# Batch 0's rotary rotations without their addition: TensorE sums both terms while it transposes, in a new order of the work

## The chip, the cores and the metric

The kernel runs on one core of a Trainium2 chip. The metric is the device time of one execution in microseconds (us). The core has five engines with queues of their own: TensorE (PE in the profile; its weight loads are shown apart, as PEld), VectorE (DVE), ScalarE (ACT), GpSimd (POOL) and SyncE (SP), which here only issues transfers. The profile gives start and duration of every instruction, and what ended each wait.

## The reference

Attention with rotary positions for 4 batches of 8 heads (576 positions, head size 64), and then an MLP with a squared ReLU:

```python
def rotate(x):
    x1, x2 = (x[..., :half], x[..., half:])
    return np.concatenate([x1 * cos - x2 * sin, x1 * sin + x2 * cos], axis=-1)
q_rot, k_rot = (rotate(q), rotate(k))
scores = scale * np.matmul(q_rot, k_rot.transpose(0, 1, 3, 2))
attn = np.exp(scores - np.max(scores, axis=-1, keepdims=True))
attn = attn / (np.sum(attn, axis=-1, keepdims=True) + 1e-09)
x = np.matmul(attn, v)           # then (B, S, H*D)
h = x @ w_in
r = np.maximum(h, 0.0)
out = (s * (r * r) + b) @ w_out
```

All inputs and the output are float32. The weights (512 x 2048 and 2048 x 512) come as 8-byte words, of which the kernel makes float32.

## The kernel before

Two heads of a batch make a pair: 16 pairs, numbers 0 to 3 for batch 0. A pair's q, k and v are loaded (`load_x`, L529) and q and k rotated. Then come, for each tile of query rows, the scores (TensorE), their maximum (VectorE), the exponential with its sum (ScalarE), a division, a transpose of the probabilities and the product with v. The MLP takes units of 256 rows as soon as their attention is there. The pairs of batches 1 to 3 are split into two float16 halves and transposed by DMA; their scores and the MLP of their rows are sums of float16 products.

Batch 0 (`FQ = (0, 1, 2, 3)`) goes another way, since the kernel starts with it: everything stays float32, and TensorE does its transposes. For a pair pr and nm = "k" or "q":

- `rotate` (L581 to L592) has three steps, each an instruction on the whole 128 x 576 tile: z = x * sin with the halves swapped (L588), x = x * cos in place (L590), x = x + z (L592). Which engine does it, VectorE or GpSimd, is in a table; for the eight rotations of batch 0 it is VectorE.
- `qk_T` (L762 to L770) transposes the 128 x 576 tile into a PSUM tile `s`: four 128 x 128 transposes (L766) and, for the last 64 columns, two 64 x 64 products with the unit matrix (L769).
- `qk_ev` copies the PSUM tile to `qkT` in SBUF on ScalarE or VectorE.
- `s_pair` (L653) makes the scores of two tiles, `s_max` (L678) their negative maxima, `s_exp` the exponentials `p`. `p_diag` and `p_T` (L794, L796) transpose and divide the probabilities, by a float32 product with a diagonal matrix.

The weights are made in the same stretch: a load (L440), one or two conversions on ScalarE, GpSimd or VectorE, a join on VectorE (L409, wio<-x), a gram of its columns on TensorE (L493) and its maximum (L496).

`plan()` (L154 on) makes a list of all pieces of work with their dependencies. It sets no order: three strings do. `ORDER` names the pieces in the order in which they are written into the program, two characters each; `PICKS` says which engine does a piece that several could do; `SLOTS` which buffer each tile takes. Every engine works through its own instructions in that order, so a piece that waits holds up what stands behind it on its engine. The buffers that matter here are two PSUM tiles for scores and transposes, and two SBUF tiles for z:

```python
BUFS = {"s": 2, "bank": 2, "po": 1, "nat": 1, "ot": 1, "xc": 4, "xt": 1, "hr": 3, "k": 2, "q": 2, "v": 4, "z": 2, "p": 4, "pab": 6, "pt": 2, "x": 4,
```

Of the kernel before, what the change touches and what calls it, by code (L numbers as in the profile page):

```python
# [7 lines left out]
F32 = mybir.dt.float32  # L8
# [20 lines left out]
B, H, S, D, DM, DFF, P = 4, 8, 576, 64, 512, 2048, 128  # L29
# [9 lines left out]
    "AAC8C9A9AMDYDZAXAyDADBDDDCA_DEDGA-DFANBADIDKAODcA4DHAPBBDJDdAiI9DLDfDMAYDeAZI-A0AaAzDgAnI_A1JFJADiARA5DOA6DhJGDmA7AkDkJB"  # L39
    "DRAcJCAjDSDjA8DlDnJDAlDTBpC-AoDPDWApBCDQASAqDUJHATDvBODXDoJIDwAbDaDVArAmAUJEJOAsAtAdDxACJJDyAVABAeAQJKJRBrBqAfJSJPAgBkJL"  # L40
    "D1BsJQAhBPBIDzDNJTBQC_DpD2D0DbBRD3JUDqBDJVEGJYDrAvAuJWDsAWADDtD4AwJdBeBmBlAEAFJXDuBnBtD5AxECJeBoBTJZBKJgBJD6JfAGBuAHBEBL"
    "A2JhBSBFAIKMBZJiA3JaEFJjBGJkEfEJJMKND_BgKPBfKOJlAJJnBhKQAKBUBVBvD7JsEAKRJmBaKSBWJNJoKWETJvBbCFEgJtJwJbKTBcJuBXJxJ7JpB0Jy"
    "BwKXEDJzEUJcJ0J2BYBxJ8EhKDJ9BdByBiKEBMBHCGCVCHKUKbJ-J1J_CIKAKFD8J3BNCbKGBjKeEIEVD9KcJqJ4B1KfALJ5KYKdEBJrKBK5B2KVKgJ6B3CX"
    "BzKhEQaaCWKiEHK6KHCKaZCYCcacD-CdB_K7abCeKlERCQB4KqadB5KjaeKZKrafKmakKsCLKkKtEKLfKIKaKnCAK8CMalLgKuFVCNELanKvCBEMC2ENKwb0"
    "LhEOamK9EPCCK-KxEEavB6aoLFapESCSKyEWKoCRLSEYayKJK0LGKpaqCTaxLHK1KCCOagC4EXC3CxawK_LTC5ahB8EZCgB7CJLCLULiCPEkLVB9LZEiKKLI"
    "LWLDaiKLKzLJLab1ajazb2b3K2LXLEarLjb4EqLKLra0Eab5a1Erb6asLkLLLsEjatLPL4CmLtElb7K3LMEtMFK4LbLNChCibGLQLAL5MGbJCzEmCjLBMHbI"
# [103 lines left out]
def plan():  # L150
# [32 lines left out]
    def prep(pr):  # L183
# [161 lines left out]
def tile_rope_attention__then__relu2_mlp(  # L345
# [755 lines left out]
```

## Time and profile before

| | |
|---|---|
| median of 3 runs | 589.58 us (588.7 to 591.73) |
| profiled execution, own time | 591.62 us |
| its span, first to last instruction | 589.8 us |
| TensorE busy | 570.6 us (97%), 4621 records |
| VectorE busy | 464.0 us (79%) |
| ScalarE busy | 417.1 us (71%) |
| GpSimd busy | 117.7 us (20%) |

A row of a timeline reads: start, busy time, engine, line, operation, out<-in by the program's names, shape, count of records [idle time of the engine before it, and what ended it]. Rows that follow each other on one line are merged. Matmuls are pipelined, so the busy time of a row reaches beyond the start of the next; the pace of a row is the distance to the next start. "L766 ... x4" is four records: a float32 product is shown as two. A wait is put down to the one that ended it last.

### The profile page before, as it was taken

What the parts mean: (1) busy time and instruction counts of PE and PEld (TensorE: products, weight loads), DVE (VectorE), ACT (ScalarE), POOL (GpSimd) and SP (SyncE); (2) the same over time, 40 slices, a digit from 0 to 9 for tenths busy, and PEclk for the clock granted to TensorE, in tenths of its full rate; (3) what the DMA queues carried; (4) which work ended last, traced back from release to release, by engine and by line L of the source; (5) the groups of instructions that cost most, each with busy time, mean ns of one, the idle gap of its engine ahead of it and who ended that gap; (6) DMA issues with size and microseconds to landing.
All of it is one profiled execution on the core that took longest, in us unless ns stands there. A gap on an engine that the chain in (4) does not pass through costs nothing.

```text
span 589.8 us, 12277 instructions
## 1 busy us (share of the span) xinstructions
PE 570.6 (97%) x4621; PEld 389.3 (66%) x4621; DVE 464.0 (79%) x975; ACT 417.1 (71%) x869; POOL 117.7 (20%) x123
## 2 busy tenths in 40 slices
PE   3799999999999999999999999999999999999997
PEld 2567867666676567666765675667656766666774
DVE  5999999999999999999999999997777464313121
ACT  4789999898999878977878786766456554443422
POOL 0146332224123541211251101201110000010000
PEclk9999999999999999999999999999999999999999
DMA  8999999987776698998647756676440334220100
GB/s 300 345 299 297 243 256 214 191 184 151 155 203 156 122 180 169 222 193 185 168 105 167 186 147 148 151 169 143 101 102 21 82 93 84 57 61 1 37 1 36
DMA packets 210011, 90.32 MB, mean 153 GB/s; under 512 B 192288, under 2 KB 196768, under 8 KB 209952
## 3 DMA queue, kind: packets, MB, share of 16 engines
q1 hardware_dynamic: 209952, 89.54, 63.5%
q8 instruction: 36, 0.59, 0.5%
q14 instruction: 23, 0.19, 0.1%
HBM read 31.97 MB, written 4.72 MB: 62 GB/s over the span
## 4 chain that ended last, share of the span: by engine, by line
PE 91%; DVE 3%; DMA 2%; ACT 2%; issue 1%; SPq 0%; DVEq 0%
PE px L889 29%; PE po L972 27%; PE px L759 9%; PE s L671 8%; PE px L922 4%; PE po L943 4%; PE s L653 3%; PE s L972 2%; DMA st_k<-in_k_dram 2%; PE po L794 1%; PE s L672 1%; PE px L493 1%; PE px L813 1%; DMA pt<-pab 1%; PE s L660 1%
## 5 line engine op out<-in xcount | busy, mean ns | idle before, releaser
L889 PE MATMUL px<-xa,wio 128*128 128x256 f16 x1536 | 179.7, 273 | 0.0
L972 PE MATMUL po<-wio,g 128*128 128x512 f16 x720 | 171.4, 379 | 0.8 <-ACT o L412 0.8
L889 PEld LDWEIGHTS <-wio 128*128 128x128 f16 x1536 | 147.7, 98 | 28.6 <-issue 2.0
L412 ACT ACTIVATE p<-s,nm 128x576 f32<-128x576 f32 x144 | 105.4, 733 | 36.0 <-DVE s L680 23.1
L972 PEld LDWEIGHTS <-g 128*128 128x128 f16 x816 | 75.8, 98 | 74.0 <-issue 3.4
L409 DVE SCALAR_TENSOR_TENSOR pab<-p,sum,pab 128x576 f16<-128x576 f32 x136 | 114.0, 849 | 7.6 <-ACT pab L412 3.7
L680 DVE TENSOR_SCALAR_CACHE_REDUCE s<-s,sc 128x576 f32<-128x576 f32 x108 | 87.9, 818 | 16.8 <-PE s L672 15.7
L406 POOL TENSOR_SCALAR pab<-p,sum 128x576 f16<-128x576 f32 x54 | 48.1, 894 | 240.5 <-DVE sum L708 189.7
L412 ACT ACTIVATE hr<-px,xc 128x512 f32<-128x512 f32 x64 | 43.7, 682 | 52.4 <-PE px L889 52.3
L913 DVE SCALAR_TENSOR_TENSOR g<-hr,xc,g 128x512 f16<-128x512 f32 x64 | 48.4, 761 | 18.8 <-ACT g L412 18.1
L412 ACT ACTIVATE pab<-p,sum 128x576 f16<-128x576 f32 x64 | 48.7, 767 | 11.0 <-DVE sum L708 10.4
L404 DVE TENSOR_SCALAR g<-hr,xc 128x512 f16<-128x512 f32 x24 | 11.9, 497 | 47.9 <-ACT hr L412 32.6
L759 PE MATMUL px<-pt,v 128*64 128x320 f16 (+2 forms) x640 | 48.9, 281 | 0.3 <-DMA pt<-pab 0.2
L412 ACT ACTIVATE hr<-hr 128x512 f32<-128x512 f32 x68 | 42.7, 628 | 1.5
L671 PE MATMUL s<-qkT 128*128 128x512 f16 (+1 forms) x120 | 41.4, 383 | 0.1
L671 PE MATMUL s<-kS,qkT 128*128 128x512 f16 (+1 forms) x120 | 41.3, 380 | 0.0
L412 ACT ACTIVATE g<-hr,xc 128x512 f16<-128x512 f32 x40 | 28.7, 717 | 16.9 <-PE po L972 10.9
L759 PEld LDWEIGHTS <-v 128*64 128x64 f16 x640 | 32.1, 110 | 11.1 <-issue 7.4
L671 PEld LDWEIGHTS <-qkT 128*128 128x128 f16 (+1 forms) x240 | 22.5, 100 | 22.8 <-issue 3.7
L922 PE MATMUL px<-x,wio 128*128 128x128 f32 x256 | 31.4, 278 | 0.0
L922 PEld LDWEIGHTS px<-x,wio 128*128 128x128 f32 x256 | 29.8, 192 | 2.2 <-issue 1.2
L412 ACT ACTIVATION_READ_ACCUMULATOR p<-s,nm 128x1 f32 x144 | 28.2, 196 | 0.0
(154 smaller groups left out, 796.3 us busy)
## 6 DMA issues: line engine op xcount, KB each, us to landing
x<-in_moe_w_in_dram SPq DMA_DIRECT2D x16, 512.0 KB, 5.1
x<-in_moe_w_out_dram SPq DMA_DIRECT2D x16, 512.0 KB, 5.0
st_v<-in_v_dram SPq DMA_DIRECT2D x16, 320.0 KB, 4.1
st_k<-in_k_dram SPq DMA_DIRECT2D x16, 288.0 KB, 3.8
st_q<-in_q_dram SPq DMA_DIRECT2D x16, 288.0 KB, 4.1
out_dram<-o SPq DMA_DIRECT2D x7, 512.0 KB, 4.2
kS<-qkT SPq DMA_DIRECT2D x24, 144.0 KB, 2.5
pt<-pab SPq DMA_TRANSPOSE x152, 2.9
```

Of the source, the lines that this page charges most:

```text
L406: eng.tensor_scalar(out=out, in0=in0, scalar1=s1, scalar2=s2, op0=op0, op1=op1)
L409: nc.vector.scalar_tensor_tensor(out=out, in0=in0, scalar=scalar, in1=in1, op0=op0, op1=op1)
L412: nc.scalar.activation(out=out, in_=in_, func=func, **kw)
L653: nc.tensor.matmul(ps[h][:, to], d["qF"][hh, t * P:(t + 1) * P], d["kF"][hh, keys], start=True, stop=True)
L671: nc.tensor.matmul(ps[rows, MAIN:2 * MAIN], lhs, kk[:, h:8:2], start=(n == 0), stop=(n == 1))
L680: nc.vector.tensor_scalar(out=T["s"], in0=T["s"], scalar1=st[pr]["es"], scalar2=None, op0=ALU.mult, op1=ALU.min, accum_out=T["nm"])
L759: nc.tensor.matmul(o[64 * h:64 * h + 64, c], v_rows(pr, h, k, z), p_rows(pr, 2 * (i // 4) + h)[:, k, c], start=((z, k) == todo[0]), stop=( ...
L889: nc.tensor.matmul(ph, w16[0][:, f, wz, cc], X["xa"][:, xz, c], start=(c == 0 and n == 0), stop=(c == NC - 1 and n == 2))
L913: nc.vector.scalar_tensor_tensor(out=g[:, 1], in0=r, scalar=xs[u]["c"][:, 2:3], in1=g[:, 0], op0=ALU.add, op1=ALU.subtract)
L922: nc.tensor.matmul(ph, wi[:, f + 1, c * P:(c + 1) * P], xs[0]["x"][:, c, j * P:(j + 1) * P], start=(c == 0), stop=(c == NC - 1))
L943: nc.tensor.matmul(X["po"][:, j * DM:(j + 1) * DM], gs["h", j, f - f % 4][:, f % 4 * P:(f % 4 + 1) * P], wo[:, f + 1], start=(n == 1), sto ...
L972: nc.tensor.matmul(po, g[:, gz, jj], w16[1][:, f, wz, to], start=(n == 1 and i == 0), stop=(n == NF and i == 2))
```

## The change

In `plan()` the rotations of batch 0 have two steps in place of three: z and x * cos are made, and x = x + z is not. z is kept as an operand of `qk_T`, which reads both tiles, so the slot of z is held until TensorE has read it. `qk_T` multiplies each block of both by the unit matrix and sums the two in PSUM: eight 128 x 128 products and four 64 x 64 ones, where four transposes and two products stood. The lines behind it move down by three (L766 becomes L768, L769 becomes L772, L794 becomes L797). The rotations of the other batches keep three steps. `ORDER`, `PICKS` and `SLOTS` are new from end to end; a line of each is shown.

```diff
 ORDER = (
-    "AAC8C9A9AMDYDZAXAyDADBDDDCA_DEDGA-DFANBADIDKAODcA4DHAPBBDJDdAiI9DLDfDMAYDeAZI-A0AaAzDgAnI_A1JFJADiARA5DOA6DhJGDmA7AkDkJB"
...
+    "AAC8C9A9AMDUDVAXAyABACADDBDCDEDDA_A-BADGAOANA4DFAPDYBBDaDHDJAQAiDZI1AZDIAYDWI2AzAaI3I9ARA0DcDbI4I-A1I_A6ADI5AnAEAFA5DeI6"
...
 PICKS = (
-    "SSSSSSGSSSGGGVGGVGGVSGVGSSSSSGSSVVSSVVSSVVSSVVSSGSGSVGGSGVVGGSVVGSSGVSSSVGGSSGVSGSVVGGSVVSGSVVGSSVGSVSVVSGSVVSGSSGSSSSSG"
...
+    "GSGGSGGGVVGGVGGGVGGSSGGVSSGSSSSSVVSSVVSSVVVSVVSSGSGGVGGSSVGGSSVVGSGVSSSVGSSSVVGGGVVGGSVVSGGVVSGGVGGSGVGSSGVGGGSSSSSSSVG"
...
 SLOTS = (
-    "000111230101000001010102003011110011011011222130001310002013113020010103100110000101010011223012310100010101110112001121"
...
+    "000111230101000010110100020131011010011102301122030010200113101010323001011200003001010110210302310001100001102011030132"
...
         for nm in "kq":
-            add((DVE, POOL), "rotate", pr, nm, steps=3, r=[("tab",)], w=[(nm, pr), ("z", pr, nm)])
+            add((DVE, POOL), "rotate", pr, nm, steps=2 if F else 3, r=[("tab",)], w=[(nm, pr), ("z", pr, nm)])
         if F:
             for nm in "kq":
-                add(PE, "qk_T", pr, nm, r=[(nm, pr), ("tab",)], w=[("s", ("T", pr, nm))])
+                add(PE, "qk_T", pr, nm, r=[(nm, pr), ("z", pr, nm), ("tab",)], w=[("s", ("T", pr, nm))])
...
-        z = new(rp, "z", [P, 9, 2, 32], F32)
+        z = st[pr]["z", nm] = new(rp, "z", [P, 9, 2, 32], F32)
...
         x, o = d[nm], new(ps_s, "s", [P, 1024], F32)
+        terms = x, d["z", nm].rearrange("p t h e -> p t (h e)")
         for t in range(4):
-            nc.tensor.transpose(o[:, t * P:(t + 1) * P], x[:, 2 * t:2 * t + 2].rearrange("p h d -> p (h d)"), ident)
-        for h in range(2):
-            hh = slice(64 * h, 64 * h + 64)
-            nc.tensor.matmul(o[hh, 512:576], x[hh, 8], ident[hh, hh], start=True, stop=True)
+            for n, y in enumerate(terms):
+                nc.tensor.matmul(o[:, t * P:(t + 1) * P], y[:, 2 * t:2 * t + 2].rearrange("p h d -> p (h d)"), ident, start=not n, stop=bool(n))
+        for n, y in enumerate(terms):
+            for h in range(2):
+                hh = slice(64 * h, 64 * h + 64)
+                nc.tensor.matmul(o[hh, 512:576], y[hh, 8], ident[hh, hh], start=not n, stop=bool(n))
         d["T", nm] = o
```

The new order shows at two places. The first is VectorE's start, from its first rotation on (st_k_109 and st_q_111 are pair 0's k and q, st_k_117 and st_q_119 pair 1's, x the weight blocks, nm the maxima of the first two score tiles). Before:

```order
L588 TENSOR_TENSOR z0_125<-st_k0_109,tab_91 128x9x2x32
L590 TENSOR_TENSOR st_k0_109<-st_k0_109,tab_91 128x576
L588 TENSOR_TENSOR z1_128<-st_q0_111,tab_91 128x9x2x32
L592 TENSOR_TENSOR st_k0_109<-st_k0_109,z0_125 128x576
L590 TENSOR_TENSOR st_q0_111<-st_q0_111,tab_91 128x576
L592 TENSOR_TENSOR st_q0_111<-st_q0_111,z1_128 128x576
L409 SCALAR_TENSOR_TENSOR wio_93<-x0_113,wio_93 128x512
L588 TENSOR_TENSOR z0_154<-st_k1_117,tab_91 128x9x2x32
L409 SCALAR_TENSOR_TENSOR wio_93<-x1_115,wio_93 128x512
L590 TENSOR_TENSOR st_k1_117<-st_k1_117,tab_91 128x576
L588 TENSOR_TENSOR z1_178<-st_q1_119,tab_91 128x9x2x32
L592 TENSOR_TENSOR st_k1_117<-st_k1_117,z0_154 128x576
```

With the change:

```order
L588 TENSOR_TENSOR z0_127<-st_k0_109,tab_91 128x9x2x32
L590 TENSOR_TENSOR st_k0_109<-st_k0_109,tab_91 128x576
L588 TENSOR_TENSOR z1_130<-st_q0_111,tab_91 128x9x2x32
L590 TENSOR_TENSOR st_q0_111<-st_q0_111,tab_91 128x576
L404 TENSOR_SCALAR wio_93<-x0_113 128x512
L409 SCALAR_TENSOR_TENSOR wio_93<-x0_113,wio_93 128x512
L409 SCALAR_TENSOR_TENSOR wio_93<-x1_115,wio_93 128x512
L588 TENSOR_TENSOR z0_169<-st_k1_117,tab_91 128x9x2x32
L588 TENSOR_TENSOR z1_176<-st_q1_119,tab_91 128x9x2x32
L590 TENSOR_TENSOR st_k1_117<-st_k1_117,tab_91 128x576
L678 TENSOR_REDUCE nm0_201<-s0_189 128x1
L409 SCALAR_TENSOR_TENSOR wio_93<-x2_121,wio_93 128x512
```

The additions L592 are gone, two weight blocks are joined ahead of pair 1's rotations, a conversion (L404) has come to VectorE, and pair 1's two z stand next to each other. z0_169 takes the slot of z0_127, z1_176 that of z1_130, and both of those are now read by TensorE.

The second place is TensorE's start. Before:

```order
L766 MATMUL s_133<-ident,st_k_109 128x128 x4
L769 MATMUL s_133<-ident,st_k_109 64x64 x2
L766 MATMUL s_144<-ident,st_q_111 128x128 x4
L769 MATMUL s_144<-ident,st_q_111 64x64 x2
L493 LDWEIGHTS wio
```

With the change, the first call alone:

```order
L768 MATMUL s_132<-ident,st_k_109 128x128
L768 MATMUL s_132<-ident,z_127 128x128
L768 MATMUL s_132<-ident,st_k_109 128x128
L768 MATMUL s_132<-ident,z_127 128x128
L768 MATMUL s_132<-ident,st_k_109 128x128
L768 MATMUL s_132<-ident,z_127 128x128
L768 MATMUL s_132<-ident,st_k_109 128x128
L768 MATMUL s_132<-ident,z_127 128x128
L772 MATMUL s_132<-ident,st_k_109 64x64 x2
L772 MATMUL s_132<-ident,z_127 64x64 x2
```

Each block's two products follow each other. Behind the two calls of pair 0 come eight grams where four stood, then the first scores and pair 1's two calls, as before. Over the whole program TensorE has 8222 instructions in place of 8174: the 48 more are the 32 and 16 products of `qk_T`.

## Rows read from the trace of the kernel before

**Rows 1.** The page: TensorE's busy time, and its granted clock in 40 slices.

```profile
PE 570.6 (97%) x4621; PEld 389.3 (66%) x4621; DVE 464.0 (79%) x975; ACT 417.1 (71%) x869; POOL 117.7 (20%) x123
...
PEclk9999999999999999999999999999999999999999
```

**Rows 2.** TensorE's waits: us in total, times, longest.

```profile
PE s L766 <- DVE st_k L592: 9.3, 1, 9.3
PE s L766 <- ACT p L412: 3.2, 2, 1.7
```

**Rows 3.** Windows: stretch, its length, busy time of PE, PEld, DVE, ACT, POOL, clock, DMA.

```profile
0.00:26.00 26.00, 13.26 (x68) 9.00 (x68) 18.96 (x32) 14.97 (x27) 1.00 (x5) 1.00 0.91 320
26.00:37.00 11.00, 9.62 (x105) 7.53 (x101) 10.57 (x22) 9.29 (x18) 3.16 (x5) 1.00 0.94 314
...
80.00:560.00 480.00, 478.35 (x3829) 319.79 (x3826) 386.07 (x819) 344.02 (x718) 92.80 (x93) 1.00 0.62 138
```

**Rows 4.** Timeline of TensorE, the first 27 us.

```profile
9.30 1.12 PE L766 MATMUL s<-ident,st_k 128*128 128x128 f32 x4 [9.30 <-DVE st_k L592]
...
13.04 2.40 PE L653 MATMUL s<-qkT 64*128 64x512 f32 x8 [0.21 <-ACT qkT L412]
17.14 1.12 PE L766 MATMUL s<-ident,st_k 128*128 128x128 f32 x4 [1.71 <-ACT p L412]
...
20.19 1.09 PE L766 MATMUL s<-ident,st_q 128*128 128x128 f32 x4 [1.52 <-ACT p L412]
...
24.61 1.11 PE L766 MATMUL s<-ident,st_q 128*128 128x128 f32 x4
25.65 0.48 PE L769 MATMUL s<-ident,st_q 64*64 64x64 f32 x4
26.07 0.72 PE L766 MATMUL s<-ident,st_k 128*128 128x128 f32 x4
26.71 0.33 PE L769 MATMUL s<-ident,st_k 64*64 64x64 f32 x4
26.98 0.86 PE L493 MATMUL px<-wio 128*128 128x128 bf16 x12
```

**Rows 5.** Timeline of TensorE, 29 to 64 us.

```profile
29.50 1.10 PE L794 MATMUL po<-dg,p 128*128 128x128 f32 x8
30.53 0.44 PE L796 MATMUL po<-dg,p 128*64 128x128 f32 x4
...
31.72 0.60 PE L766 MATMUL s<-ident,st_k 128*128 128x128 f32 x4
32.25 0.33 PE L769 MATMUL s<-ident,st_k 64*64 64x64 f32 x4
...
59.99 3.79 PE L922 MATMUL px<-x,wio 128*128 128x128 f32 x32
63.62 0.39 PE L493 MATMUL px<-wio 128*128 128x128 bf16 x4
```

**Rows 6.** Timeline of VectorE and ScalarE, 6 to 17 us.

```profile
6.36 0.76 DVE L588 TENSOR_TENSOR z<-st_k,tab 128x576 f32<-128x576 f32 x1 [5.22 <-DMA st_k<-in_k_dram]
7.15 0.76 DVE L590 TENSOR_TENSOR st_k<-st_k,tab 128x576 f32<-128x576 f32 x1
...
8.50 0.75 DVE L592 TENSOR_TENSOR st_k<-st_k,z 128x576 f32<-128x576 f32 x1
...
10.62 0.68 DVE L409 SCALAR_TENSOR_TENSOR wio<-x,wio 128x512 uint32<-128x512 uint32 x1
...
10.87 0.65 ACT L412 ACTIVATE qkT<-s 128x576 f32<-128x576 f32 x1
...
15.47 0.76 DVE L678 TENSOR_REDUCE nm<-s 128x1 f32<-128x576 f32 x1 [0.88 <-PE s L653]
...
16.26 0.74 ACT L412 ACTIVATE p<-s,nm 128x576 f32<-128x576 f32 x1 [1.03 <-DVE nm L678]
```

More of the change, by code (lines that the diff above doesn't have):

```diff
@@ new lines @@
+    "EYJUBwJ7D7J1KLBYBMByCGJ8BHBiKMBdCVCHKTJtJ2J3CIEaJ4JvBjEACbKUENB2BNJiKWJwbsALB1JxD5KVKQJjB3KXKxJ5KNJyCXKYB4EIBzCWaUB_KZKy"
+    "KdECCYaRCcEbB5CKEJaTCdKzCeaSKaD2CQKiaVJ9KeaWJ-KRKjK0J_aXKbadCACBKfKkKlaeKSCCKcKmLXKACMK1CLCRK2B6acLYEZCNEDLZafEEEiC2aYag"
+    "K3K9ahEFEKKnCSEGKoEHD8KgaiEOKsLKanKBEQKpK-aqKhKtB7J6aoK_CTKqB8apCxLLB9CJaZEParCgLMLaasCOLNLbERK6LcLRCPC4LSKCElC3K7LObtaa"
+    "KuLAK8abEjLBKrbuLPajLCKDbvEcC5LjESbwCiLdatEdbxakCzLDLkLHalCmEeLwLlEmKvLILxL9KwLTEnLyLEa_byL-K4ChEfa-EgLzbzL_LJbBEhEkb0LF"
@@ new lines @@
+    "Cya0LQEqb1bAMACjb2LGa1MBC0L3b3bCLgK5L4bDb4L0ayLmExEoLhazEyLnCrL1LiEzbJEpa2amLoEra3MGCnLpb5FMLtLqLUa4MMb6E0MHMNLrauCoL5E8"
+    "MIb7bKE9Lsb8bMLuMCMJE1b9LvE-bEb-bLLWMWLfbFMOMDbNE_L2bGbOMXb_avFPMPLeMKcAawLVFZMQB-ETCpCDMLaxCEcBEsMYCZMTCUFACkCfEuMsCaMZ"
+    "MRMaMdFLCtL6MyMeMzClcCMtMjMSL8FBE2bHMbMuMFMkL7bUM0MUMlMcE3bWE4FaCsMvMmE5bPM1E6MEcDM2CubXM5E7MVM8FCFEbVMwcEEUMfM3a5MxFFa6"
+    "bYEtcFM9a7MnM6FNM-NXbZM_EVFDbhNAMoNYNDMgNBcGNZNENacHMhM4babINbcIMiNJMpNFNcbfcJNdFOC6EWNCC1NMcKFWC7biNeNNNiMqCqNfFbCvbgFX"
@@ new lines @@
+    "NONKMrbQbjCwcSNgNLNnM7FYcTa8NoNPNqFGcUNpcVcLbRbkNQcWNjNUbSblNrGANRN1FIGbNGNsN2cMNSNVN4NHNkcNbTc4N5cObbFJFQc5cXbcNtc6NIcP"
+    "GDFHc7FRbdN6cQc8NuFSc9NyFTEvbec-GNNvc_bmFUdAN3dBFldCdDbnNTcRdEFVGOboFeN7dFbpNWcYa9OIN8cZOFNhFfdGcaNwFcdHbqcbN9OGccdQdIFd"
+    "dJcdFgdROHOJcedKNzdbdScfFmdTN-dacgdLOKPBchFoFhNlPCOAciFwPDOTOBNxOLNmdNdccjOWdUOMEwN_dlckOUOQN0dkclPEddOXcmdedMOCORONdvOV"
+    "dfGBPFOYdVF_duFKOZFicnOmdmFjOjOOdwcodOdnOnbrdWdxFnOaGPdPOoObOkODOecpPGOfcqO0OEOSFpd4O1OlcrOPd5OpPHcsOcdoOxO2dYctOddgOycu"
@@ new lines @@
+    "eMOgcvOzFxcwPNdpd6PKO3OqdXcxd7OudZO4PLO5eNO8cyOvFzFqPOOhPMO9OreOdhO6OwPPdjczdyPYO-Fyc0drGeOsdiOiF0PQO7ePPbPZGCdqPRd8FkeD"
+    "OtF1PaPcPSFrdsHpFsd9GEeCPddzQAeEc1dtFteFPeQBQDc2d1PTeGO_FuPfQEPgPjPVc3d0PJQCPkd2eHQFd-PlPWPAPyPhd3PXFvP1PzeZGFd_PIF4eBea"
+    "QGebeJF2P2PUeceAF3eQeIP3eRPieKQHedQIQoF5eLQLeeGaQpeSP0F6efeUGGegP4ehGHP5eieTP9ejGIekGJeVQJelPpP-QqPmPqemPrQRPsF8P_GKQrPo"
+    "QSenP6F7QMPneoGLQTQNPtQsPueyepGSPvQKeqQaQUerGTexPxGdP7QtfGesP8ezeWe0fFQuPwQvGMeXQwQbe1QdG0GQQze8F9QefHQ0Qfe7GZe2QcGRfIRC"
@@ new lines @@
+    "eue9QxGUQ5e-QVRDQWG3QOQge_QhQXQlGzGnREetQyQ6QQQifQF-Q7Q1QmevHsQjRFQPQYGcRTRGewQ8GoQkRHe4RUe3fJfPQnRIGpfARQQZHBfRfZRVRJRR"
+    "RNG1fSfaRORKQ9RSQ-RLRkfbGWGfe6GgRlfcRhe5GXGkfCfTfKQ2GVRmGlGhRWRXGiRbGjRiGsfERYRMRcfjQ_RjRdfUG4RyRZQ4fMQ3RBG2GmfORnRvGqRo"
+    "RzRpRAfkRsRwR0RaG5HCfBRxfDG-flRPfWR1RqfmSNGtfnSQR2fLSOR3fNfoSPfVG6GrGwfYG7fdGuG8RtSCfXG_RefeGxSRR4ffHoRfSDHNf6fhGvG9HAfp"
+    "RgSSHDftRrf7SEHGf8STfuR6HHR7f9R_fvf-R8fgf_fwgASAfifxfqRuSUgBHQfyfrHEgCfsgDR5gESYgFfzgGSBSdHFeYf0HOSFgHf2HnHIf1SGSeSKSHSg"
@@ new lines @@
+    "gISVSLHKgJShSfHLSWR9gKSIgLHYgMSuSZSXR-gwGyHRSiSaHZgTHqHaHJSjSvf3gSHrSkHbSlSJSrgUgxSsgVSMf4gWgdGYSof5SwHcHPgcIdgygNStSpTJ"
+    "gOgzTKgQgXTLTMSxSbgeSyTNS2gfHySzHSTZS3ScgmSmTOgnTaSnTPTQHdTbHTS-S0TRH1gPS_ggS1S7gRTSTAgZH2SqgoS8gbTlghS9S4gYH3TUHUTmgaTB"
+    "gpgiTVgqTigjHVTnHWHMhEg0IDHXTCTjHgTDglTGTEUBS5THTkUCHehFToHhUDTTgrS6HfTzTIhGTwTphHgkTtTxTqTFg6T0UEHzg7TWTuTrgtIbTyHigsUF"
+    "g1T1guTcTdT2TeT3UKT7T4UNICg8Tfgvg9g3UOTXT8UPg-UGg_UpTYTsUHhPhbULTvIehOhcUMhdT5TgIFg2UqUQheIPg5hfhIT9URhBhgUrhJhDIQhQThUb"
@@ new lines @@
+    "hRUYUchLT6IRUZUdhNg4hhUVHjUShihAIGhjVAhSUshkhCUThKhlUaUthmVBUuhMUeHtT-HuUfUWUjhTUgUkhnVRUIhVVSVChXUAUUUhVThUhoT_hWVUUlUy"
+    "UvVDHvh0UiHwHxUzH6H-H0hzU0UJVEH4U1VVUXH7h1VWiSU2h2hYVXiRVFH5VGU3VrVHIBVLVIhpiTIciUVJhqU4IgImU5VsU9V5hrUmU-VthZhsV6VoUnHk"
+    "U_U6V7h9VpUoUwh-U7htVqU8VahuIEiIVMUxh_h3iAhwh4VuVNhvVbiHiBVcVKVviCVzVdiJIHhyVeH8VwWQV8Vxh6hxIIVfIJV0h8iKWRiEIfiLiGWSIMWT"
+    "VgINh5InVOIKILIOVhISViVlWFV1VjVQIUh7IpiDWGiVH9ilWUWHIYVYV9iMV-imVmVkiFIVWViNiWVnVPiOWWinV_iPioWXITVyWYWCipIoicIqVZWDIhW4"
@@ new lines @@
+    "ibIiIZWEIjIkIrW5iQIWidiqiYieWZiaWbWhifW6WIV2WJigWcWiWtIXV3IlWNV4iXIuWjWOiZH_Isiwi8WdWkWKi9ivi-WuWBi_W7WLWviiWPW8ikjAW9is"
+    "jBWAjCixXSjDIvihiyjEWajFijW-jGizW_irXDi0itIyWljHXEWqjIIzi1WriujJWsWMi2Wmi4ItWwXVHlWni3WxXWjKWyhaIwW1XAXTjLHmjeW2jMWzjNjf"
+    "XXIAXUXJXYjgWeXKjhIxXZjiXjWgW0i5jyXkWfXaXFjzXbjOWpjVXBj0jjXLXCjUjPXMj1i6XlWoXgXNXOjoXhW3XPXijpXmi7XdjRjqXeYIjWYLYJjXjTYM"
+    "jYjQjrjSXnjZXGXrj2XsYKYNXxXRX6jaX7XfkQYOX8YPXyYQXtXIjcXHXoXpkRIaXzXqjkX0kSX1jmYRXQkTX9X2aEXcjbaFjdX3j8X-YTj9X_j3YAjsYBjl"
@@ new lines @@
+    "YCYFjnj-YGXuYDjtYUaBXvYHXwjuaGaCjwj_YEYqaDkAkGI0YVaHYrYnjvYsYSYojxYpkHX5YtYukBj5kIX4YvYcaIkJaMaJj7aNkKZFYykDYdj4ZGj6YzYW"
+    "ZHYwYeaKkCkLYXkdkEYZYYkeZIkfkMYakgkFkhkUkNkinykVkPkjYbkkkOklkmknkWkokpY3kYkqkXYfkZYgYhkrYiZJksYkZKYlk1ktZLYmZMkuk2kvY4Y0"
+    "lJk3k4YjZmkbZQlKnzY5kwYxkak5lTlLZNkcZOlMlUZRkxlVk_lWY6leY7n0Y8lAY9Y-Y_kzZAldk6kylfk0lgk8lNZjlOk-ZklBY1ZnlCZlk7ZoZPk9ZCZz"
+    "Y2ZSloZ0lDZBZ1lnlEZDlFlpZpZEZqZVlqlHZWn1lPlXZrZYZslGn2lIn3n4lQn5lhn6ZulxZvn7lYlyn8n9n-lSZTn_lRZUlzlZlrZXZZofl0lsZalaZblc"
@@ new lines @@
+    "lioLZcZgZdZhlkoKZioeZtZ2lbZ3lml1luogl2ljohlwoMlloNl4Z4oOl6Z5oBl8Z6ZeZ-oAZfZ7ltoCZwlvoDoVoEoFl3Z_oUo9oWoXl5ZxoYl7oZl9Z8oH"
+    "ZyaOoPoGo8aAoJo-oRaLo_oTobZ9odozopoooIoqoQoroSosoyotoiaPojoaaQocpGl-o0l_olmAo1onokmBpHmCmDmEpAommFpImGmHoumIo2owpJo3ovmJ"
+    "mKoxo5mLo4pKo6pBmwpLmxmNmymzo7pCmZmMpDmOpFmPpNmQm8mRm9pPmYmUmapEmbpMm-mcpOpRm_mkmdpQmTmlpSngmmmnmWmomSnJmpnhmXnimgnInjmf"
+    "mjmimrmumVmem0nUm1nVmsnWmvm3nXm6mhmqnAmtnBm2nKnDnLm4m7nMnEnHm5nNnCnYnFnZnOnGnQnknRnlnandnmnpnTnsncnfnvnonrnPnunSnbnxnenn"
@@ L104 @@
+    "101031530101202200511100111001110002001013122100100121121100012000221011021010"
 )
```

73 lines of the change are left out of this document (17 added, 56 removed).

## The prediction

> **What bounds the kernel now.** I read the page first [rows 1]: TensorE is busy for 570.6 of 589.8 us, and the clock row reads full from the first slice on. Then the waits of TensorE [rows 2]: 9.3 us stand before its first transpose, which waits for the third step of the first rotation (L592), and 3.2 us before two later transposes, which wait for an exponential (L412) to free a PSUM slot. The windows [rows 3] show that the rest is closed: from 80 to 560 us TensorE is busy for 478.35 of 480 us, and from 26 to 37 us it lacks 1.4 us. So what TensorE is given after the start lengthens the run by its whole price, and only the start has time to give back. There the timeline of TensorE [rows 4, 5] has a second loss: four transposes take 1.04 us (24.61 to 25.65) and later 0.53 us (31.72 to 32.25). Up to the row that begins at 26.07 us, in which the pace changes, the engine runs at the lower level, 1.2 GHz, whatever the page's clock row says; after it at 2.4 GHz. Before the rise it had worked without a pause since 20.19; the work from 9.30 to 15.4, with one pause of 0.2 us before L653, saw no rise. Of the first 26 us it was busy for 13.26 [rows 3], at half speed: that costs 6.6 us. VectorE is the other engine to read in the start, because it feeds the first transposes and is nearly always busy there [rows 6].
>
> **Part one: the third step goes.** Eight additions of 0.75 us leave VectorE (each of the eight rotations of batch 0 has it there: L592 [rows 6]). VectorE's 6.0 us are worth nothing where TensorE does not wait for it, so only two places can pay. The first is the start: k's product with cos ends at 7.15 + 0.76 = 7.91 and its addition at 8.50 + 0.75 = 9.25 [rows 6], after which TensorE began at 9.30. Now TensorE begins at about 7.95: **-1.35 us**. The other is the pause before the second pair's transposes, below.
>
> **Part two: what TensorE gets.** A call of qk_T did four 128x128 transposes and two 64x64 products with the unit matrix. It now does eight 128x128 products and four 64x64 ones. A 128x128 transpose is one record, a float32 product two: L794, four products of the same shape, counts x8 [rows 4, 5]. So a call goes from 4 to 16 records of that size, 12 more. At the upper level 32 such records (L922) take 63.62 - 59.99 = 3.63 us, 0.113 each: 12 x 0.113 = 1.36 us. The 64x64 products take 0.42 us at the lower level (25.65 to 26.07), and 0.27 at the upper one (26.71 to 26.98); doubling them adds at most that, but a part is the drain at the end of a group, which does not double (L766's four records take 0.53 where 4 x 0.113 is 0.45), so I take 0.19. Together 1.55 us a call, and **+12.4 us** for eight. The bounds: 10.9 us if the small products hide altogether, 14 if the records go at the slower pace by which L794's eight differ from L766's four ((1.03 - 0.53) / 4 = 0.125; 8 x (1.5 + 0.27) = 14.2). At the lower level the old call takes 1.46 us (24.61 to 26.07) and the new one twice 1.55 more, about 4.5, against 0.53 + 0.27 + 1.55 = 2.35 at the upper (31.72 to 32.25, and 26.71 to 26.98). Nothing hides this: no row after 37 us shows room.
>
> A rule speaks against this part. The Trainium skill, "Perfetto Trace Analysis", section Transposes, wants a transpose done as a transpose and not as a standard matmul, because it skips the arithmetic; "TensorE: Matmul & The Clock Gate", section Terms, puts the transpose mode at 4x for float32. The trace agrees with the direction and not with the factor: L794's four products take 1.03 us, L766's four transposes 0.53, not quite 2 [rows 5].
>
> **Part three: the clock.** TensorE's first work now runs without a pause from 7.95: k's call is 4.5 us long and q's follows at once. In the trace the rise came 6.0 us after the start of the unbroken work at 20.19; I take the same here, 13.95 us. Then 6.0 us run at half speed and cost 3.0 instead of 6.6: **-3.6 us**. Bounds: -4.5 if it rises after 4.2 us, and about +1 if only at 26 as before.
>
> **Part four: a new wait, and the order.** z now lives until TensorE has read it, and there are two z slots. VectorE's third z (k of pair 1) waits for TensorE's k call, the fourth (q of pair 1) for its q call; behind the fourth stand, in order, k's cos product, the first score maximum (L678), a weight join (L409) and the second maximum. I walk it with the rows: k's call ends at 12.45; q's, a third of it slow, at 15.5; the fourth z then 15.55 to 16.3, k's cos product to 17.0. The copy of q's transposes (0.65) ends at 16.2, eight weight grams fill half of that, and the scores (2.4 us slow, so about 1.2) run from 16.3 to 17.5. Maximum (0.76), exponential and release (16.26 to 17.14 in the trace, 0.88) bring pair 1's k call to 19.2, where it stood at 17.14: TensorE waits 1.7 us there, as long as the 1.71 before. q's slot is free at about 20.8, before k's call ends at 21.55, so the 1.52 us pause goes. With 0.1 us before the scores (0.21 before) that is **-1.6 us** of waits. From there 21.55 to 23.9 (q), 1.4 for p_T (29.50 to 30.53 and some 0.4 for its last rows), 0.2 for four grams, and two calls of 2.35 end at 30.2. The trace is there at 26.98, or 27.2 with the four grams that now come earlier: 3.0 late, and two calls of pair 3 add 3.1, so 6.1. The other way to add it up, 12.4 - 1.35 - 3.6 - 1.6, gives 5.85. I take **+6.0 us**.
>
> The rest of the new order moves weight conversion from ScalarE to GpSimd, reductions and normalisations between engines, and the two scalar loads to the front of SP's queue. All of that lies beside TensorE, whose list of work is otherwise the same, count for count; I cost it at nothing, covered by the closed TensorE of rows 3. If that cover goes, the pauses of 26 to 37 us show how much: 1.4 us either way.
>
> The profiled execution took 591.62 us, so the sum gives 597.6. That execution lies 2.0 us above the median of 589.58; against the median the forecast is **595.6 us**, 1.0% slower.
>
> **Rivals.** *The clock rises as late as before* (26 us). For it: the work from 9.30 to 15.4 brought no rise. Against it: that work had a pause, this has none for twice as long. The walk at the lower level: calls end at 12.45 and 16.95, grams 17.8, scores 20.2, pair 1's k 21.9 to 26.3, then fast to 35.0 at the place of 27.2: 7.8, with pair 3 10.9 late, 600.5 us.
>
> *The start closes up, and nothing is measured.* One mechanism: VectorE, free of 6.0 us, no longer lets TensorE wait. Its place is the first 37 us; its price is at most the 1.8 us of waits that my walk leaves and the 1.4 us between 26 and 37. The clock at its early bound adds 0.9, the small products hidden 1.5. It decides from 3.0 us on: then the run is within 0.5%, and all of it gives 590.0. Against it: the wait in the walk is a chain through maximum and exponential that a free VectorE does not shorten, and z now holds VectorE up.
>
> *Faster.* If a float32 product with the unit matrix were one record, like a transpose, a call would gain only 4 records and some 0.1 us, 8 x 0.55 = 4.4 us, and 4.4 - 1.35 - 3.6 - 1.6 = -2.2, with the waits of 26 to 37 gone -3.6: 586.0. It decides when a call gains less than 0.45 us. Against it stands a row: L769, in qk_T itself, is two such products with the unit matrix and counts x4.
>
> *A product costs four transposes.* Were the unit-matrix products slower than L794's, four records' time each, a call would gain 8 x 4 - 4 = 28 records instead of 12: 8 x 28 x 0.113 = 25 us in place of 10.9, about 610. L794 against L766 speaks against it [rows 5]. The factor is the one that the Trainium skill gives in "TensorE: Matmul & The Clock Gate", section Terms.
>
> **The numbers.** Forecast 0.63, its own range 593 to 598.5 (the two prices of a call, the rise 1.8 us earlier or 4 later). Clock late 0.14; closed start 0.18; one record 0.03; factor of four 0.02. About 0.5%, 2.95 us, is what a measurement of this kernel can tell from no change, so *same* ends at 592.5: faster 0.03, same 0.19, slower 0.78. Leaving out at the low end the one-record case and half the closed start, and at the top the factor of four and the worst of the late clock, the range is 591.5 to 600.5.
>
> **What would show it.** Right: L768 with 128 records where L766 had 32, 0.113 apart after the rise; TensorE's first record near 7.95; the pace doubling near 14; a wait of VectorE for TensorE before the third and fourth z; no more waits than before after 37 us; TensorE's busy time up although the slow stretch is shorter. Wrong: 64 records or fewer; a slow stretch that lasts to 26; or pauses after 37 us, which would mean that the new order, not the products, sets the time.

## The result and the profile after

| | before | changed |
|---|---|---|
| median | 589.65 us (588.7 to 591.73, 4 runs) | 594.36 us (593.87 to 594.86, 4 runs) |
| ratio of the runs | | 1.0062, 95% interval 1.0044 to 1.0081 |
| profiled execution, own time | 591.62 us | 594.60 us |
| its span | 589.8 us | 592.8 us |
| TensorE busy, records | 570.6 us, 4621 | 578.3 us, 4749 |
| VectorE busy | 464.0 us | 466.7 us |

The changed kernel is slower, by 4.7 us of the medians and 3.7 us by the ratio. It was forecast at 595.6, 6.0 more. A second set of runs of the same two kernels (below, e12) gave a ratio of 1.0061.

Pairs are called by their place in the order here, as ahead of this: the second to be transposed is called pair 1 and the third pair 2. In the program these two carry each other's number, since `ORDER` takes batch 0's pairs as 0, 2, 1, 3, in both kernels. This matters for one experiment (e6).

TensorE's waits in the changed kernel, us in total, times and longest, answer to [rows 2]:

```profile
PE s L768 <- DVE st_k L590: 7.4, 1, 7.4
PE s L768 <- ACT p L412: 1.7, 1, 1.7
PE px L493 <- DVE wmx L496: 1.4, 1, 1.4
PE po L797 <- ACT dg L412: 0.4, 1, 0.4
PE s L653 <- ACT qkT L412: 0.2, 1, 0.2
```

And the windows (stretch, length, busy time of PE, PEld, DVE, ACT, POOL, granted clock, DMA), which answer to [rows 3]:

```profile
0.00:26.00 26.00, 16.75 (x135) 14.92 (x136) 16.97 (x34) 11.41 (x21) 3.22 (x8) 0.93 0.85 293
26.00:37.00 11.00, 11.00 (x122) 9.47 (x121) 8.74 (x21) 6.29 (x13) 1.95 (x4) 1.00 0.93 316
37.00:80.00 43.00, 42.58 (x443) 33.35 (x441) 41.06 (x87) 39.04 (x87) 23.43 (x26) 1.00 0.95 267
80.00:560.00 480.00, 478.62 (x3837) 320.59 (x3837) 393.97 (x835) 343.65 (x717) 97.23 (x91) 1.00 0.64 139
```

The row of the kernel before for 37 to 80 us, for comparison:

```profile
37.00:80.00 43.00, 43.00 (x433) 33.58 (x433) 42.17 (x95) 41.43 (x97) 20.71 (x20) 1.00 0.99 273
```

Between the two profiled executions the span grew by 3.0 us. TensorE is busy for 7.7 us more and idle for 4.7 us less (589.8 - 570.6 = 19.2, now 592.8 - 578.3 = 14.5). The idle time that went lies in the start: 1.9 us before the first record (9.30, now 7.37), 1.6 us of pauses up to 26 us (26 - 9.30 - 13.26 = 3.4, now 26 - 7.37 - 16.75 = 1.9), and 1.4 us between 26 and 37 us, where no pause is left. After 37 us the idle time is the same within 0.1 us, but its places changed: a pause of 0.4 us before L797 at 55 us and one of 1.4 us before L493 at 141 us are new or longer, and shorter ones went.

The timeline of TensorE in the start answers to [rows 4, 5]. L768 is the large products, two records a row and term; of pair 0's and pair 1's calls the first and the last rows stand here:

```profile
7.37 0.80 PE L768 MATMUL s<-ident,st_k 128*128 128x128 f32 x2 [7.37 <-DVE st_k L590]
...
9.66 0.63 PE L768 MATMUL s<-ident,z 128*128 128x128 f32 x2
10.09 0.45 PE L768 MATMUL s<-ident,st_k 128*128 128x128 f32 x2
10.37 0.39 PE L768 MATMUL s<-ident,z 128*128 128x128 f32 x2
...
11.06 0.49 PE L768 MATMUL s<-ident,st_q 128*128 128x128 f32 x2
...
13.43 0.64 PE L493 MATMUL px<-wio 128*128 128x128 bf16 x8
14.25 1.30 PE L653 MATMUL s<-qkT 64*128 64x512 f32 x8 [0.18 <-ACT qkT L412]
17.25 0.80 PE L768 MATMUL s<-ident,st_k 128*128 128x128 f32 x2 [1.71 <-ACT p L412]
...
20.40 0.42 PE L768 MATMUL s<-ident,z 128*128 128x128 f32 x2
...
21.12 0.49 PE L768 MATMUL s<-ident,st_q 128*128 128x128 f32 x2
...
23.48 1.16 PE L797 MATMUL po<-dg,p 128*128 128x128 f32 x8
...
29.86 0.86 PE L493 MATMUL px<-wio 128*128 128x128 bf16 x12
```

A call at the upper level runs from 21.12 to 23.48, 2.36 us. The pace doubles at 10.1 us, 2.7 us after the first record; after the pause of 1.71 us it is at the lower level again (two records from 17.84 to 18.27, 0.43 us) and doubles again at 20.4. Pair 2's second call ends at 29.86, where the trace of before stood at 26.98, or 27.2 with the four grams that now come earlier: 2.7 us late.

VectorE waits for TensorE where a z slot is used again. Of pair 1's two z the second, q's, waits for 1.60 us; before the first, k's, no wait shows:

```profile
11.18 0.76 DVE L588 TENSOR_TENSOR z<-st_k,tab 128x576 f32<-128x576 f32 x1
13.54 1.15 DVE L588 TENSOR_TENSOR z<-st_q,tab 128x576 f32<-128x576 f32 x1 [1.60 <-PE s L772]
14.61 0.74 DVE L590 TENSOR_TENSOR st_k<-st_k,tab 128x576 f32<-128x576 f32 x1
15.57 0.76 DVE L678 TENSOR_REDUCE nm<-s 128x1 f32<-128x576 f32 x1 [0.22 <-PE s L653]
```

### The profile page after: what moved, and what is told of

It is laid out like the page before. It is cut to its first block, busy times and chain, and to the rows that moved or that the text cites. A ratio compares the mean times of both kernels' runs of the same rounds, so it can differ in the third digit from the quotient of the medians.

```text
span 592.8 us, 12553 instructions
## 1 busy us (share of the span) xinstructions
PE 578.3 (98%) x4749; PEld 399.9 (67%) x4749; DVE 466.7 (79%) x981; ACT 410.2 (69%) x851; POOL 125.8 (21%) x127
## 4 chain that ended last, share of the span: by engine, by line
PE 94%; DVE 2%; DMA 2%; ACT 1%; issue 0%; SPq 0%; DVEq 0%; ACTq 0%
PE px L892 28%; PE po L975 26%; PE px L759 9%; PE s L671 8%; PE px L925 5%; PE po L946 5%; PE s L768 3%; PE s L653 3%; PE s L975 2%; PE s L672 1%; DMA x<-in_moe_w_in_dram 1%; PE po L797 1%; PE px L493 1%; DMA st_k<-in_k_dram 1%; PE s L660 1%; PE s L772 1%
## 5 line engine op out<-in xcount | busy, mean ns | idle before, releaser
L409 DVE SCALAR_TENSOR_TENSOR pab<-p,sum,pab 128x576 f16<-128x576 f32 x136 | 115.8, 862 | 6.3 <-POOL pab L406 2.7
L406 POOL TENSOR_SCALAR pab<-p,sum 128x576 f16<-128x576 f32 x47 | 44.5, 948 | 248.4 <-DVE sum L708 196.6
L412 ACT ACTIVATE pab<-p,sum 128x576 f16<-128x576 f32 x71 | 53.4, 766 | 7.6 <-DVE sum L708 5.9
L404 DVE TENSOR_SCALAR g<-hr,xc 128x512 f16<-128x512 f32 x25 | 12.6, 503 | 41.2 <-ACT hr L412 26.6
L759 PEld LDWEIGHTS <-v 128*64 128x64 f16 x640 | 32.1, 110 | 10.8 <-issue 6.7
L678 DVE TENSOR_REDUCE nm<-s 128x1 f32<-128x576 f32 x36 | 26.2, 748 | 4.2 <-PE s L653 3.0
```

The costliest lines, as they stand in the source:

```text
L406: eng.tensor_scalar(out=out, in0=in0, scalar1=s1, scalar2=s2, op0=op0, op1=op1)
L409: nc.vector.scalar_tensor_tensor(out=out, in0=in0, scalar=scalar, in1=in1, op0=op0, op1=op1)
L412: nc.scalar.activation(out=out, in_=in_, func=func, **kw)
L678: nc.vector.tensor_reduce(out=T["nm"], in_=T["s"], axis=AX.X, op=ALU.max, negate=True)
L759: nc.tensor.matmul(o[64 * h:64 * h + 64, c], v_rows(pr, h, k, z), p_rows(pr, 2 * (i // 4) + h)[:, k, c], start=((z, k) == todo[0]), stop=( ...
```

## The experiments

Theory A: TensorE's added records set the time, against which the start gives something back. Theory B: the new order costs it. Theory C: the new order held the loss down. Runs of one kernel spread over 1 to 4 us, so the verdicts go by the ratio to the kernel before on the same chip.

**e1: the arithmetic in the old order.** The order, engines and slots of before; the third step issues nothing.

```diff
         yield
-        eng.tensor_tensor(out=x, in0=x, in1=z, op=ALU.add)
+        if not (pr in FQ):
+            eng.tensor_tensor(out=x, in0=x, in1=z, op=ALU.add)
...
```

`qk_T` sums two products a block for batch 0, as in the change.

> The change's arithmetic alone, in the order of before: the third step of batch 0's rotations is empty and qk_T sums two products a block; order, engines and slots are those of before. Theory A (TensorE's added records set the time): eight calls at 1.55 us are 12.4 us, less 1.35 us of earlier start and 3 to 4 us of the slow stretch, with the pauses of before left as they are: 594 to 597 us. Theory B (the new order, not the products, costs the 4.7 us): within 1 us of before, 589 to 591. Theory C (the new order is what held the loss down): over 598.

Measured: 595.76 us, ratio 1.0087 (1.0070 to 1.0103). The products alone, with nothing moved, cost 5.1 us: theory A, and B falls. So does C, which asked for over 598. The changed kernel's ratio, 1.0061 and 1.0062, lies below e1's by about 1.5 us, but the intervals overlap, also with that of e4 on the same chip (1.0056 to 1.0084). That the new order gave something back is therefore likely and not shown by the times. In the profiled executions e1's span is 1.4 us longer than the change's (594.2 against 592.8). TensorE's idle time is the same there, 14.5 us. Its 4749 records take 1.3 us longer (579.6 against 578.3): 0.5 in the calls of `qk_T`, of which more ran at the lower pace, and 0.8 in the same other records in their old succession.

One row of e1 matters for what follows. In the old order, too, no pause is left between 26 and 37 us:

```profile
26.00:37.00 11.00, 11.00 (x123) 9.43 (x122) 8.85 (x17) 7.82 (x17) 1.31 (x2) 1.00 0.86 292
```

**e2: the order without the arithmetic.** In the changed kernel the addition is issued with the second step and `qk_T` is that of before.

```diff
         eng.tensor_tensor(out=x, in0=x, in1=cos, op=ALU.mult)
+        if pr in FQ:
+            eng.tensor_tensor(out=x, in0=x, in1=z, op=ALU.add)
...
```

> The new order alone: the addition is back, as a third VectorE instruction right behind the cos product, and qk_T transposes one tile again. Theory A: TensorE's list is that of before, so 589 to 591 us, with a slow stretch as long as before. Theory B: the loss stays, 593 to 595. Theory C: under 587.

Measured: 598.48 us, ratio 1.0136 (1.0121 to 1.0152). None of the three: TensorE has the list of before and takes 8.0 us more. TensorE's timeline and VectorE's at the place:

```profile
24.84 0.63 PE L768 MATMUL s<-ident,st_q 128*128 128x128 f32 x4 [1.19 <-issue]
...
28.01 1.08 PE L768 MATMUL s<-ident,st_k 128*128 128x128 f32 x4 [2.29 <-issue]
...
29.44 1.04 PE L493 MATMUL px<-wio 128*128 128x128 bf16 x8
```

```profile
23.65 1.09 DVE L592 TENSOR_TENSOR st_q<-st_q,z 128x576 f32<-128x576 f32 x1
...
26.83 1.08 DVE L592 TENSOR_TENSOR st_k<-st_k,z 128x576 f32<-128x576 f32 x1
```

The profile names no releaser for these two pauses ("issue"), but the additions end at 24.74 and 27.91, and TensorE's transposes begin 0.1 us behind each: the new order leaves no room for a third step. After the pause of 2.29 us TensorE runs at the lower level again (1.08 for four transposes), and in the window from 26 to 37 us the granted clock is 0.69 where it was 1.00. So e2 does not price the order. It shows that the new order goes with two steps and not with three, and that a pause can cost the level with it.

**e3: only pair 0's calls sum products**, in the old order (the condition of e1 is `pr == 0`).

> In the order of before, only pair 0's two rotations lose their addition and only its two calls of qk_T sum products; pairs 1 to 3 are as before. Theory A with cover: the two calls' 3.1 us lie ahead of the pause of 1.7 us in which TensorE waits for pair 0's exponential, TensorE starts 1.35 us earlier and the pace doubles before the scores, so pair 1's first transpose stays at 17 us: 589 to 590.5 us. If nothing covers them: 3.1 - 1.35 = 1.7 us more, 591.4 us. If the early rise is kept to the end of the start: under 587.

Measured: 592.44 us, ratio 1.0035 (1.0022 to 1.0047), 2.1 us more, where 1.7 were expected without any cover. The cover was not there: in its profile the scores (L654 here) began at 16.35, where they stood at 13.04 [rows 4], and pair 1's first call behind the same pause of 1.71 us at 19.35 in place of 17.14:

```profile
16.35 1.30 PE L654 MATMUL s<-qkT 64*128 64x512 f32 x8 [0.41 <-ACT qkT L412]
19.35 0.66 PE L777 MATMUL s<-ident,st_k 128*128 128x128 f32 x4 [1.71 <-ACT p L412]
```

The pause moves with the calls, since it is a chain from the scores through maximum and exponential; it does not absorb them.

**e4: no wait for z.** In the changed kernel pair 0's z lie in a buffer that is first used later.

```diff
-        z = st[pr]["z", nm] = new(rp, "z", [P, 9, 2, 32], F32)
+        if pr == 0:
+            if "zz" not in vs:
+                vs["zz"] = pp.tile([P, 1440], F32, tag="pt1", name="pt1", bufs=1)
+            n = 576 * "kq".index(nm)
+            z = st[pr]["z", nm] = vs["zz"][:, n:n + 576].rearrange("p (t h e) -> p t h e", t=9, h=2)
+        else:
+            z = st[pr]["z", nm] = new(rp, "z", [P, 9, 2, 32], F32)
```

> The changed kernel, with pair 0's two z in a buffer that is not used until later, so that VectorE does not wait for TensorE before pair 1's z. The wait costs nothing (pair 1's first call waits for the exponential of pair 0's scores, which does not hang on z): 594 to 595 us. The wait costs its 1.6 us: under 593.2. Theory A holds in both cases; only the price of the new wait is asked.

Measured: 594.42 us, ratio 1.0070 (1.0056 to 1.0084): unchanged. VectorE's wait went elsewhere:

```profile
11.85 0.75 DVE L594 TENSOR_TENSOR z<-st_q,tab 128x576 f32<-128x576 f32 x1
12.51 1.23 DVE L596 TENSOR_TENSOR st_k<-st_k,tab 128x576 f32<-128x576 f32 x1
16.73 0.76 DVE L684 TENSOR_REDUCE nm<-s 128x1 f32<-128x576 f32 x1 [2.99 <-PE s L659]
```

z is early (the second of pair 1's at 11.85, where it began at 13.54), and VectorE waits 2.99 us for the scores instead. The new wait was free, as expected.

**e9: the changed kernel without z's large products.** The sine term of the first 512 positions of batch 0 is left out; the small products of z stay, and with them every wait for z.

```diff
-            for n, y in enumerate(terms):
-                nc.tensor.matmul(o[:, t * P:(t + 1) * P], y[:, 2 * t:2 * t + 2].rearrange("p h d -> p (h d)"), ident, start=not n, stop=bool(n))
+            for n, y in enumerate(terms[:1]):
+                nc.tensor.matmul(o[:, t * P:(t + 1) * P], y[:, 2 * t:2 * t + 2].rearrange("p h d -> p (h d)"), ident, start=True, stop=True)
```

> The changed kernel without the four 128x128 products of z in each call: the sine term of the first 512 positions of batch 0 is left out. z is still read by the 64x64 products, so every wait of VectorE stays; a call has 8 records fewer, 8 x 0.113 = 0.9 us at the upper level. Theory A: 7.2 us less over eight calls, less what the slow stretch and the pauses take back in the start (up to 2 us): 587 to 589.5 us. If the records were hidden: 594.

Measured: 589.98 us, ratio 0.9982 (0.9972 to 0.9993), so 0.8% or 4.7 us under the changed kernel (3.3 to 6.0 by the ends of the two intervals), and half a microsecond above the range that was expected. 64 records of 0.113 us are 7.2 us, of which about two thirds came out. The profiled executions agree: TensorE is busy for 7.5 us less (570.9 against 578.3) and idle for 1.9 us more, so a part turned into pauses. TensorE waits at 20.80 (0.62), at 22.87 (0.55) and again at 31.75 (0.32) where it had no pause, and from 26 to 37 us it is busy for 10.24 us, not 11.00:

```profile
26.00:37.00 11.00, 10.24 (x106) 8.09 (x103) 10.29 (x22) 7.95 (x16) 4.72 (x6) 1.00 0.98 350
```

VectorE is as free of the third step here as in the change, and the order is the new one. With fewer records TensorE runs into VectorE, ScalarE and the weight blocks again. So it is the added records that fill the pauses of 26 to 37 us, in the new order as in the old one (e1). That is the room in which the change hid part of its price.

**e11: the same price after the start.** The kernel before, with 50 score products of batches 1 to 3 issued twice.

```diff
+    twice = []
...
+            if i < 8 and len(twice) < 50:
+                twice.append(i)
+                nc.tensor.matmul(ps[rows, MAIN:2 * MAIN], lhs, kT[:, h:8:2], start=True, stop=True)
             for n, kk in enumerate((kT, kS)):
```

> The kernel before with TensorE's list made longer after the start: 50 score products of batches 1 to 3 (128x512, float16, 216 ns apart) are issued twice, the second overwriting the first: 10.8 us more work and no other change. If TensorE has no room after the start, the whole price shows: 600 to 602 us against 590.6. If part of it is hidden beside VectorE: under 598.

Measured: 601.51 us, ratio 1.0175 (1.0160 to 1.0191), 10.3 us for 10.8 of records. After the start nearly the whole of a record is paid; in the start, by e9, about two thirds.

**e12: the changed kernel again.**

> The changed kernel once more, unaltered, to stand beside the others on one chip: 594 to 595.5 us.

Measured: 594.73 us, ratio 1.0061 (1.0049 to 1.0073). Its profile shows another start: the pace doubles at about 12.5 and holds over the same pause of 1.71 us:

```profile
12.45 0.48 PE L768 MATMUL s<-ident,z 128*128 128x128 f32 x2
...
18.40 0.49 PE L768 MATMUL s<-ident,st_k 128*128 128x128 f32 x2 [1.71 <-ACT p L412]
```

**e5, e6, e8, e10: the pace raised by itself.** TensorE multiplies a block of ones by itself from 1.05 us on (64 products in e5 and e6, 52 in e8, 84 in e10), and in e6, e8 and e10 again behind the first scores (24, 24 and 30); nothing reads the results. e6 has 20 more behind a later call. e8 is the changed kernel, the others the kernel before.

```diff
+    def idle_work(n):
+        o = po_tile()
+        for i in range(n):
+            nc.tensor.matmul(o[:, 0:P], ones16b, ones16b, start=True, stop=True)
...
+        idle_work(64)
```

> The kernel before with 64 bfloat16 products of a block of ones by itself on TensorE from the first microsecond on, into a PSUM tile that nothing reads; about 7 us at the lower pace, done before the first transpose. If the slow start is what the change partly repaired, raising the pace without any price gains: the first transposes and scores run in half the time, pair 1's first call comes some 1.7 us earlier: 587 to 589 us against 590. If the pace falls again in the pauses before pair 1's calls, only that. If the slow stretch costs nothing because VectorE and the loads set the start: 590.

Measured: 590.71 us, ratio 0.9989 (0.9975 to 1.0003): no difference that can be told, so the first expectation falls. The second, that the pace falls again before pair 1's calls, is what the profile shows; what it left can't be told from nothing. Its profiled execution, at 588.48 among the shortest of its runs (588.13 to 592.27), shows what a higher level gives and what takes it back:

```profile
8.09 0.66 PE L766 MATMUL s<-ident,st_k 128*128 128x128 f32 x4 [1.56 <-DVE st_k L592]
...
11.81 1.30 PE L653 MATMUL s<-qkT 64*128 64x512 f32 x8 [1.00 <-ACT qkT L412]
15.39 1.11 PE L766 MATMUL s<-ident,st_k 128*128 128x128 f32 x4 [2.29 <-ACT p L412]
```

Transposes and scores run in about half the time, but the waits for ScalarE grow (1.00 where 0.21 stood, 2.29 where 1.71), and behind the longer pause the level has fallen (1.11 for four).

> As the run before it, with 24 such products behind the first scores and 20 behind pair 1's k call, where TensorE waits for exponentials (1.71 and 1.52 us), so that no pause is longer than about half a microsecond. If the pace is then held, the whole 6.6 us at half speed are gone, of which the chain through VectorE and ScalarE keeps some: 584.5 to 587.5 us. If the start is bound by VectorE and the loads: 588 to 590.

Measured: 592.30 us, ratio 1.0023 (1.0008 to 1.0038): slower, and outside both expectations. The edit doesn't do what was expected of it. It puts the 20 products behind the k call of the pair that the program numbers 1, the third in the order, and not into the pause of 1.52 us before the second pair's q call:

```profile
20.50 0.63 PE L766 MATMUL s<-ident,st_q 128*128 128x128 f32 x4 [1.02 <-ACT p L412]
...
28.05 1.28 PE L1003 MATMUL po<-ones16b 128*128 128x128 bf16 x20 [1.34 <-ACT pt L412]
```

So the pause stayed (1.02 us), and the 20 products, which write the PSUM tile of p_T, waited 1.34 us for its copy. In the profiled execution, moreover, the first transpose came only at 9.90, after a pause of 3.06 us, and the 24 products behind the first scores ran at the lower level (2.74 us). e6 tells nothing of the level held.

> The changed kernel with 52 such products at the start and 24 behind the first scores. It had 5.9 us at half speed, and its calls are longer, so TensorE is closer to setting the start itself: 3 us less if TensorE sets it, 591 to 592 us; unchanged at 594 if the chain through maximum and exponential does. In both cases it stays above the kernel before treated alike by what its added records cost less the earlier start.

Measured: 592.06 us, ratio 1.0027 (1.0017 to 1.0037), 2 us under the changed kernel, about what was expected if TensorE sets the start. Here the level holds from the first call on, and pair 1's call begins at 16.15 in place of 17.25:

```profile
7.05 0.49 PE L768 MATMUL s<-ident,st_k 128*128 128x128 f32 x2 [1.51 <-DVE st_k L590]
...
14.38 1.51 PE L1006 MATMUL po<-ones16b 128*128 128x128 bf16 x24
16.15 0.49 PE L768 MATMUL s<-ident,st_k 128*128 128x128 f32 x2 [0.26 <-ACT p L412]
```

Even without any slow call the changed kernel stays above the unaltered kernel before, by 1.6 us.

> The kernel before with 84 products of ones at the start instead of 64, so that the pause ahead of the first transpose is about 1 us shorter, and 30 behind the first scores; none behind pair 1's k call. If the level is held into pair 1's calls, as in the changed kernel treated so: 587 to 589 us. If the first loads land so late that the pause before the first transpose stays long, the level falls again: 590 to 591.

Measured: 589.96 us (588.42 to 592.27), ratio 0.9981 (0.9968 to 0.9994): 1.1 us under the kernel before, by ratio the lowest of all that leave nothing out, by little. It lies between the two expectations, and the profile has some of either: pair 1's k call comes at 15.19 and at the upper level, but its q call still waits 2.14 us for an exponential, and from the products behind its transposes (18.80) until 22.36 the lower pace is back:

```profile
18.24 0.63 PE L766 MATMUL s<-ident,st_q 128*128 128x128 f32 x4 [2.14 <-ACT p L412]
18.80 0.47 PE L769 MATMUL s<-ident,st_q 64*64 64x64 f32 x4
```

## Why the prediction was right

The measured 594.36 lies in the likeliest case, 593 to 598.5, 1.2 us from its value. The mechanism is the forecast one: TensorE's added records set the time (e1, e9, e11), and the start gives a part of it back. The size of the change was forecast too large, 6.0 us against 3.7 by the ratio. The terms of the sum beside the two profiled executions, in us:

| | forecast | measured |
|---|---|---|
| idle before the first record | -1.35 | -1.9 |
| TensorE's busy time (12.4 of products, -3.6 of the clock) | +8.8 | +7.8 |
| pauses up to 26 us | -1.6 | -1.6 |
| pauses from 26 to 37 us | 0 | -1.4 |
| idle after 37 us | 0 | +0.1 |
| sum | +5.85 | +3.0 |

These two executions lie closer together than the medians do, because the one of the kernel before is the slowest of its four runs. Point by point:

- *What TensorE gets*: right. L768 has 128 records, 0.112 us apart at the upper level; a call takes 2.36 us, 2.35 were forecast. That nothing after the start hides it is shown by e11.
- *The rule on transposes* held in direction, by the pace: a product is two records, 0.22 us, a transpose 0.13 to 0.15 (four from 31.72 to 32.25 in the kernel before, four from 8.09 to 8.68 in e5). e1, 0.9% slower, doesn't test it by itself, since a call there has also twice as many products as it had transposes. A factor of 4 a product would have shown as 28 more records' time a call; the calls show 12 and the small products.
- *The third step goes*: right for the reason given, TensorE's first record follows k's cos product. It came at 7.37, not 7.95, because k landed earlier (z began at 5.76, 6.36 before). That is a difference between executions: the same load lets TensorE begin at 6.78 to 7.99 in the runs e1, e3, e4, e9 and e12.
- *The clock*: the sum right, its course wrong. The rise was taken at 6.0 us after the first record; it came after 2.7 us in one execution and about 5 in another (in e3 after about 6), and the forecast had no fall. In the first one the slow work is 2.7 + 3.15 = 5.9 us, with the fall counted; 6.0 were forecast. That they agree so closely is luck: the slow work is about 4.9 us in e12, and 7.3 in e1 (3.7 and, after the pause, 3.6). The case of a clock as late as before did not come.
- *The new wait*: right that it is there (1.60 us) before the fourth z, and that pair 1's call waits for the exponential for as long as before, 1.71. A wait before the third z was named as well and does not show. That the z wait costs nothing was only implied; e4 shows it.
- *The step that was mis-sized* is the price of the products: each of the eight calls was to lengthen the run by its whole 1.55 us, also those of pairs 2 and 3 between 26 and 37 us, where TensorE had pauses. At the end of pair 2's calls walk and trace agree (2.7 late, 3.0 forecast; the call ends at 29.50 to 29.86 in the change, e1, e4 and e12). But the pauses of 26 to 37 us, 1.4 us, which the forecast read and left in place, are filled by the added records: they are gone in e1, without the new order, and back in e9, with the new order and 64 records fewer. The forecast had made them a matter of the new order, with either sign.
- *The rest of the new order*, costed at nothing, gave no idle time back beyond that. It has a small effect on busy time. Counted from the start of a record to the next, the calls of `qk_T` went from 10.0 to 21.6 us; batch 0's scores, p_T and the grams lost 3.3, since fewer of them ran at the lower pace; all other records lost 0.5. e1, with the same records in the old order, lost 0.2 of this last part. The earlier first load, 0.6 us, is the other part of the difference, and chance.
- *The rivals*: the closed start came true in part, in that the pauses after 26 us went. Its mechanism, VectorE free of 6.0 us, is not enough: in e9 VectorE is as free, and TensorE waits there. One record a product and four transposes a product are ruled out by the record counts and the 2.36 us.

## What to carry to other kernels

Where one engine has no idle time left from some point to the end, ask of every edit what it adds to that engine, and pay it in full there. In the kernel's first stretch, where engines take turns, only part is paid, because added work fills pauses that the engine had: count these pauses into the sum. Taking 6 us from an engine that is busy but not waited for bought little: about 1.3 us at the first record, beside 0.6 from the load, against 12.4 us of new work on the engine that sets the time. An order that was searched for one set of steps is not a neutral place to test another: e2's 8 us are no price of anything but that.

## What the runs showed of the hardware

TensorE's level is not the same from one execution of a kernel to the next: in the changed kernel it rose at 10.1 us and fell in a pause of 1.71 us in one execution, and rose at 12.5 and held through the same pause in another, with spans of 592.8 and 592.4 us. In e5 a pause of 2.29 us ended at the lower level; in e10 one of 2.14 us ended with four transposes at the upper level and the next products at the lower. The profile's clock row of the kernel before reads full in the first 26 us, in which the paces show half; the pace of equal records is the surer sign. Raising the level with work of no use gained 2 us in the changed kernel (e8), and in the kernel before nothing clear (e5) or 1.1 us (e10): there the waits for ScalarE grew instead (2.29 us where 1.71 stood in e5, 2.14 where 1.52 stood in e10).
